# A layout of modes with batches innermost, and mixing matmuls of 64 columns

## The chip, the core and the metric

The kernel runs on one core of one Trainium2 chip. The metric is device time in microseconds for one call: the median of 3 runs is 380.75 us (380.23, 380.75 and 383.44).

## The reference

x is (8, 5696, 128), h (5696, 128), w_r and w_i (64, 128, 128), w_ch (128, 128). First a long convolution of x with h along the sequence, then a spectral mix of the lowest 64 frequencies, then a channel layer with a residual:

```python
# _attn_ref: L = 2 * S
y = irfft(rfft(x, n=L, axis=1) * rfft(h, n=L, axis=0)[None], n=L, axis=1)[:, :S]
# _moe_ref, with x = y of above
X = rfft(x, axis=1);  Xr, Xi = real(X[:, :64]), imag(X[:, :64])
Yr = einsum('bmd,mde->bme', Xr, w_r) - einsum('bmd,mde->bme', Xi, w_i)
Yi = einsum('bmd,mde->bme', Xr, w_i) + einsum('bmd,mde->bme', Xi, w_r)
u = x + irfft(Yr + 1j * Yi on the lowest 64 modes, n=S, axis=1)
return u + maximum(u @ w_ch, 0)
```

## The kernel before, in words

The program is written as one list of operations by a recorder (`R.add`), which keeps for every engine the order in which the operations are recorded and works out the semaphore waits from the buffers and PSUM banks that each one reads and writes. Reads of one PSUM bank by two engines are put in sequence too. So nothing is reordered on an engine: what the code writes first on ScalarE or VectorE runs first there. Matmuls go through `mm` (line 320), evictions of PSUM through `evac` (lines 308 to 314), DMAs through `dma` (line 317).

The sequence is cut into 89 blocks of 64 positions, and the batch into four pairs (`g_`, 0 to 3). The stages in order:

1. 57 warm-up matmuls; then the transform of h along the blocks (`Hp`, `Ah`), and its filter values (`Hs`).
2. For each pair: the transform of x (`a_tile`, written to `As`), and a loop of ticks (`tick`): `second` makes the spectrum from `As` and the table `M`, `products` multiplies it with `Hs`, `third` transforms back in part, evicts to `Zs` or `Zt` and writes that to DRAM (`zscr`), and `modes_of` sums the 64 modes of the mix in PSUM bank 7 (`MB`).
3. At the end of each pair, lines 702 to 705 evict the modes from bank 7 to the tile `XT`. For every batch it has three pieces of 64 columns: minus the imaginary part, the real part, the imaginary part (`XTW` = 192 columns a batch). The first eviction writes the last two pieces for both batches (256 elements a partition), the second the negated one (128). Both are on ScalarE for the first three pairs; in the last, the second is on VectorE.
4. After the last pair, the mix (`mix`, line 773): for each mode m two matmuls with weights of w_r and w_i from the tile `W`, accumulated in PSUM. The moving operand of 16 columns takes, for one mode, two pieces of XT times eight batches, 64 and 192 elements apart. Modes 0 to 31 go to bank 6 and 32 to 63 to bank 7.
5. Between the parts of the mix stand transform matmuls of the output stage that do not need its result (`u_z(..., True)`, 89 columns each, reading `ZT0` and `S4`). They take banks 0 to 5 by the list `LSLOT`. Two reflections (lines 771 and 772), one on VectorE (S4a) and one on ScalarE (S4b), are recorded ahead of the mix.
6. Y is evicted in two halves (line 786): bank 6 on ScalarE, bank 7 on VectorE, 512 elements each. Eight transposes (line 791) turn it, into banks 6 and 7; two evictions write `C`.
7. The output stage: `u_tile` adds C times the table `IBs` (356 columns a matmul) and the transform of `ZT` chunks (five buffers, 1,440 KB a chunk, loaded from `zscr`) to a tile `UT`; `o_tile` makes u @ w_ch next to u, ScalarE the relu, VectorE the sum, SyncE's queue stores it. Chunks are loaded again into a ZT buffer when its matmuls are done.

Of the kernel before, what the change touches and what calls it, by code (L numbers as in the profile page):

```python
# [4 lines left out]
P = 128  # L5
# [8 lines left out]
RELU = mybir.ActivationFunctionType.Relu  # L14
# [109 lines left out]
def bass_long_conv_fft__then__afno_spectral_mix_kernel(nc, x, h, moe_w_r, moe_w_i, moe_w_ch, out):  # L124
    B, S, D = x.shape
    M = moe_w_r.shape[0]
# [122 lines left out]
    XTW = 3 * M  # L249
    xt = at("XT", B * XTW, F16, a_g + GW * 2 + 2048 * (NZX - NZ))  # L250
# [24 lines left out]
    NR = len(r_off)  # L275
    r_sb = [at(f"R{i}", 512, F32, r_off[i]) for i in range(NR)]
    w_sb = at("W", 2 * M * D, F16, a_x)
    y_sb = at("Y", 2 * B * M, F16, r_off[0])
# [10 lines left out]
    def pv(bank, off, dims, p0=0, n=P):  # L289
        return bass.AP(ps, p0 * 4096 + bank * 512 + off, [[4096, n]] + [list(d) for d in dims])  # L290

    R = Recorder(nc)
# [3 lines left out]
    def bank(i):  # L296
        return ("bank", i)
# [3 lines left out]
    def evac(dst, src, reads, writes, scale=None, eng=None, after=()):  # L301
        e = eng
        if e is None:
            turn[0] ^= 1
            e = "scalar" if turn[0] else "vector"
        if e == "scalar":
            if scale is None:
                R.add(e, lambda h_: h_.copy(dst, src), reads, writes, after=after)  # L308
            else:
                R.add(e, lambda h_: h_.activation(dst, src, COPY, scale=scale), reads, writes, after=after)  # L310
        elif scale is None:
            R.add(e, lambda h_: h_.tensor_copy(dst, src), reads, writes, after=after)  # L312
        else:
            R.add(e, lambda h_: h_.tensor_scalar_mul(dst, src, scale), reads, writes, after=after)  # L314
# [4 lines left out]
    def mm(o, l, r, st, sp, reads, writes):  # L319
        R.add("tensor", lambda h_: h_.matmul(o, l, r, start=st, stop=sp), reads, writes)  # L320
# [3 lines left out]
    def once(key, toks):  # L324
        if key in first:
            return []
        first[key] = 1
        return list(toks)
# [72 lines left out]
    MB = 7  # L401
# [14 lines left out]
    for j in range(16):  # L416
        t = turns("h", [0, 2, 4])
        for i in range(8):
            d = 8 * j + i
            for r in range(2):  # L420
# [6 lines left out]
             eng="vector" if j % 4 == 1 else "scalar")  # L427
# [90 lines left out]
    def reflect(eng, t, n, col, key, after):  # L518
        MN = S - SH
        dst, src = bass.AP(t, SH, [[S, n], [1, MN]]), bass.AP(t, SH - NQ - 1, [[S, n], [-1, MN]])  # L520
        sc = sg_sb[0:n, col:col + 1]
        if eng == "scalar":
            R.add(eng, lambda e: e.activation(dst, src, COPY, scale=sc), [key + (0,), ("sg",)], [key + (1,)], after=after)
        else:
            R.add(eng, lambda e: e.tensor_scalar_mul(dst, src, sc), [key + (0,), ("sg",)], [key + (1,)], after=after)
# [153 lines left out]
    for g_ in range(NP):  # L679
        for t in range(NT + LM if g_ + 1 == NP else NT):  # L680
            if g_ == 0 and t % 2 == 0 and t // 2 < NG:
                load_g(t // 2)
            tick(g_, t)
            assert g_ + 1 < NP or not wp
            if g_ == NP - 1 and t in early:
                pace[:] = [("u", min(t, NT - 1) % NU)] if t else []
                early[t]()
        if g_ + 1 < NP:
            load.update(scalar=600.0, vector=0.0)
            third(g_, NT - 2)  # L690
            a_tile(0, [0], share(720))
            a_tile(1, [2], share(720))
            third(g_, NT - 1)
            load["scalar"] += 560.0
            a_tile(2, [0], share(720))
            modes_of(g_, NT - 3)
            a_tile(3, [4], share(720))
            modes_of(g_, NT - 2)
            a_tile(4, [2], share(720))
            modes_of(g_, NT - 1)  # L700
            load["scalar"] += 700.0
        evac(bass.AP(xt, 2 * g_ * XTW + M, [[B * XTW, P], [XTW, 2], [1, P]]), pv(MB, 0, [[P, 2], [1, P]]),
             [bank(MB)], [("xt", g_)], 1.0 / 64, eng="scalar", after=[("ag", k) for k in range(NS + 2 * XN, NK)])
        evac(bass.AP(xt, 2 * g_ * XTW, [[B * XTW, P], [XTW, 2], [1, M]]), pv(MB, M, [[P, 2], [1, M]]),
             [bank(MB)], [("xtn", g_)], -1.0 / 64, eng="vector" if g_ + 1 == NP else "scalar", after=[("ag", k) for k in range(NS + 2 * XN, NK)])
        if g_ + 1 < NP:
            for j in range(5, 32):
                a_tile(j, [(0, 4, 6, 2)[(j - 5) % 4]], "both" if j == 31 else share(720))
                if j == 31:
                    idle(4, 2)  # L710
                if wp and j % 2 == 1:
                    dst, src_, ring, tok = wp.pop(0)
                    dma("gpsimd", dst, src_, ring, (), [tok], after=[("as", j)])
# [56 lines left out]
    XTT = [(n, g_) for g_ in range(NP) for n in ("xt", "xtn")]  # L770
    reflect("vector", s4_sb[0], P, 0, ("s4", 0), M_ALL[1:4])
    reflect("scalar", s4_sb[1], PB + RB, 1, ("s4", 1), AST)
    def mix(m0, m1):
        for m in range(m0, m1):
            for ri, first_col in ((0, M + m), (1, m)):
                mm(pv(6 + m // 32, m % 32 * 2 * B, [[1, 2 * B]]), w_sb[:, (ri * M + m) * D:(ri * M + m + 1) * D],
                   bass.AP(xt, first_col, [[B * XTW, P], [M, 2], [XTW, B]]), ri == 0, ri == 1, WT + XTT, [bank(6 + m // 32)])

    u_z(0, 0, 0, True)
    for n in range(2):  # L780
        mix(16 * n, 16 * n + 16)
        u_z(0, 0, 1, True, (n,))
    mix(32, M)
    u_z(0, 1, 0, True, (0,))
    for hb in range(2):
        evac(bass.AP(y_sb, hb * 32 * B, [[2 * M * B, P], [B, 32], [M * B, 2], [1, B]]),
             pv(6 + hb, 0, [[2 * B, 32], [B, 2], [1, B]]), [bank(6 + hb)], [("y", hb)], eng="vector" if hb else "scalar",
             after=ZY)
    for b in range(B):
        bk = 6 + b // 4  # L790
        R.add("tensor", lambda e, b=b, bk=bk: e.transpose(  # L791
            ps16[:, bk * 1024 + (b % 4) * P:bk * 1024 + (b % 4) * P + P], bass.AP(y_sb, b, [[2 * M * B, P], [B, P]]), id_sb[:, :]),
              [("y", 0), ("y", 1), ("id",)], [bank(bk)])
    u_z(0, 1, 0, True, (1,))
    for hb in range(2):
        evac(c_sb[:, hb * 512:hb * 512 + 512], ps16[:, (6 + hb) * 1024:(6 + hb) * 1024 + 512], [bank(6 + hb)],
# [11 lines left out]
    def o_tile(g_, b, r4):  # L808
        ub = (g_ % 2) * 2 + b
        bb = 2 * g_ + b  # L810
        t = turns("l", LSLOT)
        i = n_o[0]
        n_o[0] += 1
        full = r4 < NW // 4
        last_ = (g_, b) == (NP - 1, 1)
        wide = r4 < (8 if last_ else NW // 4 // 2 * 2)
        big = wide or (last_ and full)
        h_ = r4 % 2 if wide else 0
        if big:
            if not h_:  # L820
                o_cur[0] = turns("o8", list(range(NO8)))
            ob, key, old = o8_sb[o_cur[0]], ("o8", o_cur[0]), o8_old[o_cur[0]]
        else:
            k_ = turns("os", list(range(NO)))
            ob, key, old = o_sb[k_], ("os", k_), o_old[k_]
        OW = 1024 if big else 512
        n, rows = (4, P) if full else (1, TAIL)
        rd = [("u_", ub, c_) for c_ in range(2 * NCH)] + [("wch",), ("i16",)]
        for j in range(n):
            lh = bass.AP(u_sb[ub], 4 * r4 + j, [[S, P], [NW, P]]) if full else u_sb[ub][:, NW * P:S]  # L830
            mm(pv(t + j // 2, (j % 2) * 256, [[1, 256]], 0, rows), lh, WI, True, True, rd, [bank(t + j // 2)])
        bk = [bank(t), bank(t + 1)] if full else [bank(t)]
        rs = r_sb[i % NR]
        rv = bass.AP(rs, 0, [[512, rows], [P, n], [1, P]])
        ov = bass.AP(ob, h_ * 512, [[OW, rows], [P, n], [1, P]])
        src_r, src_u = pv(t, 0, [[256, n], [1, P]], 0, rows), pv(t, P, [[256, n], [1, P]], 0, rows)
        R.add("scalar", lambda e: e.activation(rv, src_r, RELU), bk, [("r", i % NR)], after=once(("r", i % NR), G_ALL + XTT + [("y", 0), ("y", 1), ("id",)]))  # L837
        R.add("vector", lambda e: e.tensor_tensor(ov, src_u, rv, ADD), bk + [("r", i % NR)],  # L838
              [key + (h_,)], after=once(key, old))
        if wide and not h_:  # L840
            return
        w_ = (2 if wide else 1) * 4 * D
        if full:
            dst = bass.AP(out.tensor, out.offset + bb * S * D + (4 * r4 - 4 * h_) * D, [[NW * D, P], [1, w_]])
            src = ob[:, 0:w_]
        else:
            dst = bass.AP(out.tensor, out.offset + bb * S * D + NW * P * D, [[D, TAIL], [1, D]])
            src = ob[0:TAIL, 0:P]
        dma("sync", dst, src, "o", [key + (v_,) for v_ in range(h_ + 1)])
# [53 lines left out]
```

## Time and profile before

| what | before |
|---|---|
| median of 3 runs | 380.75 us (380.23 to 383.44) |
| the profiled execution's own time | 383.51 us |
| its span, first to last instruction | 381.7 us |
| its mean granted TensorE clock | 0.933 |
| busy PE / PEld / DVE / ACT / POOL | 363.6 / 280.4 / 303.7 / 311.9 / 83.9 us |
| the mix: first and last of 128 matmuls start | 257.7 and 262.1 us |
| eviction of Y: ScalarE, VectorE | 585 and 693 ns |
| evictions of XT: 256 elements, 128 elements on ScalarE | 379 and 285 ns (mean) |
| the eight transposes | 263.16 to 264.21 us |
| first and last matmul that reads C (IBs) start | 264.6 and 366.0 us |

The page gives busy time by engine, the span in 40 slices, the chain of work that ended last and the costliest groups. PE is the matmul row, PEld the loading of weights (it overlaps PE), DVE is VectorE, ACT ScalarE, POOL GpSimd, SP SyncE. PEclk is the granted clock of TensorE as a share of full speed. In a line such as `257.70 5.23 PE ps L320 x152` of the chain, the numbers are the start and the length in us, then engine, tile and line, and how many instructions were merged. The times inside the trace are of the profiled execution, which is 2.8 us above the median of the runs.

### The profile page before, as it was taken

To read this page: it belongs to the slowest core of one execution; us is meant where nothing else is said; L and a number is where in the kernel's file an instruction comes from. 1 tells how busy PE (TensorE), PEld (TensorE's weight loads), DVE (VectorE), ACT (ScalarE), POOL (GpSimd) and SP (SyncE) were. 2 spreads that over 40 slices of the span, in tenths; PEclk is the share of its full clock that TensorE was granted. 3 is DMA by queue.
4 is the path that set the end of the run, shared out by engine and by line. 5 is a ranking of instruction groups with operands and counts; after the bars stand their busy time and mean duration, and the time that the engine had idled before them with its cause. 6 is when DMAs were issued, how large, how long until landed. Compare 5 with 4: busy or idle time off the path is not lost.

```text
span 381.7 us, 11950 instructions
## 1 busy us (share of the span) xinstructions
PE 363.6 (95%) x5107; PEld 280.4 (73%) x5107; DVE 303.7 (80%) x331; ACT 311.9 (82%) x492; POOL 83.9 (22%) x137
## 2 busy tenths in 40 slices
PE   7998989999989999999999899999999999999992
PEld 4898856667856667766668666668898988888871
DVE  7566998998988998889998888766347766777784
ACT  8357989998989998999998899994466777777783
POOL 8400012320823311822203211339000000000000
PEclk9997999999999999999999999996899999999997
DMA  7998589998999996999996599999999999999867
GB/s 137 201 280 349 140 228 227 276 269 238 107 134 228 234 269 167 143 129 250 235 283 119 137 298 251 300 328 406 407 388 402 402 415 414 404 408 378 342 256 313
DMA packets 84560, 103.92 MB, mean 272 GB/s; under 512 B 22126, under 2 KB 68974, under 8 KB 81538
## 3 DMA queue, kind: packets, MB, share of 16 engines
q1 hardware_dynamic: 59643, 67.73, 51.3%
q0 software_dynamic: 24864, 35.43, 44.3%
q8 instruction: 40, 0.66, 0.7%
q14 instruction: 13, 0.11, 0.1%
HBM read 70.61 MB, written 51.12 MB: 319 GB/s over the span
## 4 chain that ended last, share of the span: by engine, by line
PE 82%; ACT 9%; DVE 6%; issue 1%; DMA 0%; DVEq 0%
PE ps L320 82%; ACT As L310 7%; DVE As L314 2%; DVE U L597 1%; DVE Hs L312 1%; ACT R L837 0%; DMA F<-cF 0%; DVE UT L312 0%; ACT UT L308 0%; ACT XT L310 0%; DVE O L838 0%; PE ps L791 0%; ACT Hs L308 0%; DVE Os L838 0%; ACT Ah L310 0%
## 5 line engine op out<-in xcount | busy, mean ns | idle before, releaser
L320 PE MATMUL ps<-U,Wc 128*128 128x512 f16 (+1 forms) x368 | 95.8, 384 | 0.0
L605 DVE TENSOR_TENSOR U<-Xs,Hs 128x2048 f16<-128x2048 f16 (+1 forms) x68 | 80.7, 1189 | 11.5 <-ACT Xs L308 10.0
L308 ACT CAST Xs<-ps 128x1024 f16<-128x1024 f32 (+1 forms) x72 | 69.5, 971 | 7.8 <-PE ps L320 4.8
L838 DVE TENSOR_TENSOR O<-ps,R 128x512 f32<-128x512 f32 x81 | 52.5, 686 | 19.8 <-ACT R L837 12.5
L308 ACT CAST Zs<-ps 128x512 f16<-128x512 f32 (+1 forms) x126 | 66.0, 604 | 0.0
L837 ACT ACTIVATE R<-ps 128x512 f32<-128x512 f32 x96 | 50.9, 573 | 14.6 <-PE ps L320 14.1
L314 DVE TENSOR_SCALAR As<-ps 128x720 f16<-128x720 f32 (+1 forms) x60 | 50.1, 879 | 9.1 <-PE ps L320 8.0
L310 ACT ACTIVATE As<-ps 128x720 f16<-128x720 f32 (+1 forms) x72 | 51.6, 772 | 6.6 <-PE ps L320 5.7
L320 PE MATMUL ps<-F,Xin 128*128 128x180 f16 x512 | 54.5, 255 | 2.6 <-ACT Ah L310 1.0
L320 PEld LDWEIGHTS ps<-F,Xin 128*128 128x128 f16 x512 | 46.8, 156 | 9.3 <-DVE As L314 2.6
L320 PE MATMUL ps<-WI,UT 128*128 128x256 f16 x360 | 52.5, 281 | 0.5 <-DVE O L838 0.4
L320 PE MATMUL ps<-As,M 64*128 64x128 f16 x1440 | 48.9, 217 | 4.3 <-DVE U L597 3.5
L320 PEld LDWEIGHTS ps<-U,Wc 128*128 128x128 f16 x368 | 28.5, 98 | 28.5 <-ACT Zs L308 6.1
L320 PEld LDWEIGHTS ps<-As,M 64*128 64x128 f16 x1440 | 40.5, 94 | 10.9 <-DVE U L597 4.2
L317 POOL DMA_DIRECT2D Xt<-in_x_dram x48 | 24.8, 520 | 102.9 <-PE ps L320 102.2
L605 DVE TENSOR_TENSOR U<-ps,Hs 128x2048 f16<-128x2048 f32 x20 | 45.7, 2283 | 0.0
L308 ACT CAST UT<-ps 128x712 f16<-128x712 f32 x40 | 30.0, 752 | 18.7 <-PE ps L320 18.7
L320 PEld LDWEIGHTS ps<-WI,UT 128*128 128x128 f16 x360 | 39.5, 152 | 4.4 <-issue 2.2
L320 PE MATMUL ps<-IBs,C 128*128 128x356 f16 x128 | 40.8, 328 | 0.4
L320 PEld LDWEIGHTS ps<-G,Zs 128*128 128x128 f16 x492 | 27.3, 97 | 13.3
L308 ACT CAST Zt<-ps 128x512 f16<-128x512 f32 (+1 forms) x58 | 31.0, 606 | 0.1
L320 PE MATMUL ps<-G,Zs 128*128 128x2 f16 (+2 forms) x492 | 30.5, 192 | 0.0
(88 smaller groups left out, 500.3 us busy)
## 6 DMA issues: line engine op xcount, KB each, us to landing
out_dram<-O SPq DMA_DIRECT2D x39, 512.0 KB, 10.4
zscr<-Zs SPq DMA_DIRECT2D x60, 256.0 KB, 6.3
Xt<-in_x_dram POOLq DMA_DIRECT2D x24, 320.0 KB, 6.9
zscr<-Zt SPq DMA_DIRECT2D x28, 256.0 KB, 6.6
W<-wscr POOLq DMA_DIRECT2D x8, 512.0 KB, 5.3
M<-cM POOLq DMA_DIRECT2D x5, 720.0 KB, 20.3
ZT0a<-zscr SPq DMA_DIRECT2D x3, 1024.0 KB, 13.4
Xr<-in_x_dram POOLq DMA_DIRECT2D x8, 320.0 KB, 13.8
```

What stands on the lines that cost most here:

```text
L308: R.add(e, lambda h_: h_.copy(dst, src), reads, writes, after=after)
L310: R.add(e, lambda h_: h_.activation(dst, src, COPY, scale=scale), reads, writes, after=after)
L312: R.add(e, lambda h_: h_.tensor_copy(dst, src), reads, writes, after=after)
L314: R.add(e, lambda h_: h_.tensor_scalar_mul(dst, src, scale), reads, writes, after=after)
L317: R.add(eng, lambda h_: h_.dma_start(dst, src), reads, writes, ring=ring, after=after)
L320: R.add("tensor", lambda h_: h_.matmul(o, l, r, start=st, stop=sp), reads, writes)
L597: R.add("vector", lambda e, b=b, s_=s_: e.tensor_tensor(bass.AP(u_s[i], b * 512, [[2048, P], [1024, 2], [1, n * D]]), s_, hv, MULT), [tok, ...
L605: R.add("vector", lambda e: e.tensor_tensor(uv, src, hv, MULT), bk + [("h", t, 0), ("h", t, 1, 0), ("h", t, 1, J)], [("u", i)])
L837: R.add("scalar", lambda e: e.activation(rv, src_r, RELU), bk, [("r", i % NR)], after=once(("r", i % NR), G_ALL + XTT + [("y", 0), ("y", 1 ...
L838: R.add("vector", lambda e: e.tensor_tensor(ov, src_u, rv, ADD), bk + [("r", i % NR)], [key + (h_,)], after=once(key, old))
```

## The change

The tile XT is laid out with batches innermost: each mode has 24 columns, eight for minus the imaginary part, eight for the real part, eight for the imaginary part. The evictions at the end of each pair write the same elements to the new places, so each element lands 48 bytes from the next mode's. A mixing matmul now reads its 16 columns side by side. It reads them four times over (a step of 0) and writes 64 columns, the four copies 64 columns apart in its bank. Only the first copy of a mode is used. Later modes of the same bank write over the copies that lie in their place. The modes are spread over four banks, 4 to 7, 16 modes a bank, instead of two. Y is evicted in quarters, ScalarE and VectorE in turn, each as soon as its 16 modes are recorded, and the transposes wait for all four.

```diff
-        evac(bass.AP(xt, 2 * g_ * XTW + M, [[B * XTW, P], [XTW, 2], [1, P]]), pv(MB, 0, [[P, 2], [1, P]]),
+        evac(bass.AP(xt, 2 * g_ + B, [[B * XTW, P], [1, 2], [B, 2], [3 * B, M]]), pv(MB, 0, [[P, 2], [M, 2], [1, M]]),
...
-        evac(bass.AP(xt, 2 * g_ * XTW, [[B * XTW, P], [XTW, 2], [1, M]]), pv(MB, M, [[P, 2], [1, M]]),
+        evac(bass.AP(xt, 2 * g_, [[B * XTW, P], [1, 2], [3 * B, M]]), pv(MB, M, [[P, 2], [1, M]]),
...
+    MQ = M // 4
+
     def mix(m0, m1):
         for m in range(m0, m1):
-            for ri, first_col in ((0, M + m), (1, m)):
-                mm(pv(6 + m // 32, m % 32 * 2 * B, [[1, 2 * B]]), w_sb[:, (ri * M + m) * D:(ri * M + m + 1) * D],
-                   bass.AP(xt, first_col, [[B * XTW, P], [M, 2], [XTW, B]]), ri == 0, ri == 1, WT + XTT, [bank(6 + m // 32)])
+            for ri, first_col in ((0, B), (1, 0)):
+                mm(pv(4 + m // MQ, m % MQ * 2 * B, [[8 * B, 4], [1, 2 * B]]), w_sb[:, (ri * M + m) * D:(ri * M + m + 1) * D],
+                   bass.AP(xt, m * 3 * B + first_col, [[B * XTW, P], [0, 4], [1, 2 * B]]), ri == 0, ri == 1, WT + XTT, [bank(4 + m // MQ)])
+
+    def y_out(q):
+        evac(bass.AP(y_sb, q * MQ * B, [[2 * M * B, P], [B, MQ], [M * B, 2], [1, B]]),
+             pv(4 + q, 0, [[2 * B, MQ], [B, 2], [1, B]]), [bank(4 + q)], [("y", q)], eng="vector" if q % 2 else "scalar",
+             after=ZY)
 
     u_z(0, 0, 0, True)
     for n in range(2):
-        mix(16 * n, 16 * n + 16)
+        mix(MQ * n, MQ * n + MQ)
+        y_out(n)
         u_z(0, 0, 1, True, (n,))
-    mix(32, M)
+    for n in range(2, 4):
+        mix(MQ * n, MQ * n + MQ)
+        y_out(n)
     u_z(0, 1, 0, True, (0,))
-    for hb in range(2):
-        evac(bass.AP(y_sb, hb * 32 * B, [[2 * M * B, P], [B, 32], [M * B, 2], [1, B]]),
-             pv(6 + hb, 0, [[2 * B, 32], [B, 2], [1, B]]), [bank(6 + hb)], [("y", hb)], eng="vector" if hb else "scalar",
-             after=ZY)
     for b in range(B):
...
-              [("y", 0), ("y", 1), ("id",)], [bank(bk)])
+              [("y", q) for q in range(4)] + [("id",)], [bank(bk)])
```

More of the change, by code (lines that the diff above doesn't have):

```diff
@@ L836, in o_tile @@
         src_r, src_u = pv(t, 0, [[256, n], [1, P]], 0, rows), pv(t, P, [[256, n], [1, P]], 0, rows)
-        R.add("scalar", lambda e: e.activation(rv, src_r, RELU), bk, [("r", i % NR)], after=once(("r", i % NR), G_ALL + XTT + [("y", 0), ("y", 1), ("id",)]))
+        R.add("scalar", lambda e: e.activation(rv, src_r, RELU), bk, [("r", i % NR)], after=once(("r", i % NR), G_ALL + XTT + [("y", q) for q in range(4)] + [("id",)]))
         R.add("vector", lambda e: e.tensor_tensor(ov, src_u, rv, ADD), bk + [("r", i % NR)],
```

## The prediction

> **What bounds the kernel now.** I read the page first. TensorE is busy for 95% of the span and carries 82% of the chain that ended last.
>
> ```profile
> span 381.7 us, 11950 instructions
> PE 363.6 (95%) x5107; PEld 280.4 (73%) x5107; DVE 303.7 (80%) x331; ACT 311.9 (82%) x492; POOL 83.9 (22%) x137
> PEclk9997999999999999999999999996899999999997
> PE 82%; ACT 9%; DVE 6%; issue 1%; DMA 0%; DVEq 0%
> ```
>
> The clock row says more than the busy row: the granted clock dips in slice 4 (about 29 us), in slices 28 and 29 (about 262 us), and at the end, when PE is done. The second dip lies at the mixing stage, which is what the change edits. So next I read the chain of waits from 254 us on, in order of time.
>
> ```profile
> 256.53 1.03 PE ps L320 x18
> 257.56 0.15 issue
> 257.70 5.23 PE ps L320 x152
> 262.93 0.23 issue
> 263.16 1.05 PE ps L791 x8
> 264.21 29.32 PE ps L320 x437
> ```
>
> TensorE is the path without a break: what it loses here, the end loses. The 152 are the 128 mixing matmuls and 24 of the transform; L791 are the eight transposes. Then the view by windows, once per clock window.
>
> ```profile
> 254.80:258.20 3.40, 3.23 (x59) 2.55 (x58) 0.89 (x2) 3.03 (x7) 3.40 (x5) 0.95 1.13 362
> 258.20:261.60 3.40, 3.40 (x113) 3.40 (x110) 2.92 (x1) 2.21 (x2) 3.40 (x4) 0.95 1.05 427
> 261.60:265.00 3.40, 3.17 (x52) 2.85 (x49) 1.45 (x3) 0.60 (x1) 3.40 (x5) 0.50 1.01 398
> 265.00:268.40 3.40, 3.40 (x25) 2.30 (x24) 1.34 (x2) 1.41 (x2) 2.97 (x3) 0.50 1.07 388
> 268.40:271.80 3.40, 3.40 (x64) 3.00 (x63) 1.80 (x2) 1.09 (x2) 0.00 (x0) 0.94 1.05 418
> ```
>
> Columns: stretch, length, busy PE, PEld, DVE, ACT, POOL, granted clock, DMA share, GB/s. From 261.6 to 268.4 us the clock is 0.50 instead of 0.95, though PE was busy for all of the window ahead of it. In the trace's clock records the first dip runs from 29.51 to 32.92 us (3.413 us) and the second from 261.62 to 268.44 (6.827, twice that); they start 232.107 us apart, 68.0 times 3.413. So the clock is decided in steps of 3.413 us.
>
> What decides it? I counted, in each step, the columns that the started matmuls read (their number times their width). 258.2 to 261.6 has 92 of 16 and 16 of 89, that is 2,896, and the clock falls after it. 26.1 to 29.5 has 3,420, and it falls. 254.8 to 258.2 has 4,040, and it stays; every other step between 29.5 and 370 us has more. At half clock, 261.6 to 265.0 has 3,464 and the clock stays low; 265.0 to 268.4 has 3,916 and it rises. So one limit between 3,464 and 3,916 columns per step fits every step of this trace. The mixing matmuls are many but narrow, and fall under it. The view of the tile XT has them:
>
> ```profile
> L320 PE MATMUL ps<-XT,W x128: 187/192/194, 257.7 to 262.1; 128*128 128x16 f16 x128
> L310 ACT ACTIVATE XT<-ps x7: 285/374/383, 94.5 to 256.8; 128x256 f16<-128x256 f32 x4, 128x128 f16<-128x128 f32 x3
> L314 DVE TENSOR_SCALAR XT<-ps x1: 292/292/292, 257.3 to 257.3; 128x128 f16<-128x128 f32 x1
> ```
>
> **Part by part, against the profiled execution's 383.51 us** (span 381.7 and 1.8 around it).
>
> *The mixing matmuls.* Same 128, same weights; 64 columns instead of 16. Start to start they take 29.8 ns now, at either clock, so width does not set it. Rows around it at 0.95: 2 or 4 columns 27 ns, 89 columns 43, 128 columns 55. 64 columns at that clock stream in 28 ns; with the 3 that the 89-wide ones show on top, 31. Cost 128 x 1.2 = +0.15 us; bounds 27 (-0.36) and 43 (+1.7), and I take 31 because the 128-wide row shows no overhead at all.
>
> *The clock.* In the profile's step 258.2 to 261.6 there would be 92 x 64 + 1,424 = 7,312 columns. Ahead of it 4,040 + 18 x 48 = 4,904. Behind it some 18 x 64 + 16 x 89 + 8 x 128 and six of 356, about 5,700. All clear 3,916, so the dip at 261.6 should not come, at whatever phase the steps lie.
>
> *From the last mixing matmul (262.14) to the first that reads C (264.61), 2.47 us now.* The last Y eviction halves: 693 ns for 512 elements on VectorE, 414 for 256 (the Hs eviction's row). Then 0.23 to its start, 0.41, 0.10 to the first transpose, three transposes at 55 instead of 107 ns (0.17), 0.25 until their result is there, 0.60 for C on ScalarE, 0.05: 1.81 us. -0.66. PE's own work in it (8 transposes, 16 of 89 columns) takes about 1.1 and hides.
>
> *From 264.61 to 268.44, at half clock:* 9 matmuls of 356 columns and 16 of 89. Behind the dip they take 154 and 43 ns: 2.07 instead of 3.84 us, -1.77. VectorE's C, IBs reflection and first UT eviction (0.42, 0.93, 0.90 in a row) free banks 0 and 1 about 2.85 us after the first transpose, and PE wants them after 3.0: covered, narrowly.
>
> *Y in four pieces.* All four are waited for by the transposes, and behind these stand all later matmuls. The first lies on ScalarE behind the S4b reflection (ends 259.83), the second on VectorE behind S4a's (ends 261.12); at 0.41 each they are done by 261.6, before the last mixing matmul, and so are banks 4 and 5 for the transform matmuls that now reuse them. Nothing.
>
> *The XT evictions* keep their number and size but write single 2-byte elements 48 bytes apart. Two at each of three boundaries and two at 256.8 are on the chain. Nearest row: As evictions with 4-byte pieces, 512 ns (ACT) and 533 (DVE) for 360 elements, where a line through contiguous rows (Zs 614 for 512, Xs 1017 for 1024) gives 494: 4% more. At 4%, +0.06 us in all. Upper bound: the element part doubles, 0.3 per boundary, +1.2. Nothing suggests a gain.
> [...]
>
> *What is late next.* DMA share is 1.0 from 255 to 345 us, so transfers do not come earlier with PE. ZT3b lands at 273.64 and is first read at 276.37; ZT4b 277.63 and 280.31: 2.7 us to spare. PE about 2 us earlier uses that up, and the reload of ZT0 (issued 268.34 when PE has freed it) starts 2 us sooner and shares the engines with them. 0 to +1.0; I take +0.3.
>
> Sum: 0.15 - 0.66 - 1.77 + 0.06 + 0.3 = -1.92: the profiled execution would take 381.6.
>
> **From there to the median.** The profiled execution is 2.8 us above the median of 380.75, beside the highest run (383.44). Two things depend on where the steps fall: whether the gap near 28.5 to 29.5 brings the early dip (the change leaves it alone), and how long the later dip lasts. The narrow stretch (about 255.4 to 262.3) is longer than a step, so each phase has at least one low step; the dip's end then falls between 265.7 and 269.1. Each us behind 264.61 costs 1.77/3.84 = 0.46, so the clock term lies between 0.5 and 2.1. The lower runs are likelier short dips: end at 266.5, 0.87, with 0.1 for DMA. 0.15 - 0.66 - 0.87 + 0.06 + 0.1 = -1.2. Forecast 379.5 us.
>
> **Rivals.**
> *The clock falls all the same (slower).* The trace shows columns with a clock, not that a column read four times counts four times. If only new data or results count, the mixing step still has 2,896 and the dip stays; but now 64 columns at half clock take 53 ns (half of the transposes' 107), 23.5 more than now. The dip starts between 258.9 and 262.3 by phase, so 10 to 100 of the 128 pay: +0.2 to +2.3, less 0.28 for Y. It decides as soon as the counted columns stay below 3,464. Middle: 381.8. Against it, from the trace: the 57 warm-up matmuls read 180 columns twice each; the step up to 5.62 us has 11 of them, 3,960 columns in full and 1,980 if a repeat counts nothing, and the clock rose. For it: those were twice, these are four times 16, and a count of another kind that fits all steps is not excluded.
> [...]
>
> *The dip goes, but transfers hide the gain.* ZT3b and ZT4b come late by a us: 379.5 + 0.9 = 380.4. For it: the DMA share of 1.0. Against: 2.7 us to spare.
>
> *XT's writes cost their double.* 379.5 + 1.1 = 380.6. For it: no row has pieces of 2 bytes. Against: pieces of 4 bytes cost 4%. [...]
>
> *More than forecast.* If the timed runs carry the long dip and the steps after it never dip again, the gain is 2.5 to 3, and with luck in the early dip 376.5.
>
> **How the numbers follow.** Forecast 0.62 (378.2 to 380.0), clock falls 0.10, transfers 0.08, XT 0.08, more 0.12. The range from 377.4 to 382.0 leaves out the best of the last and the worst of the first rival. About 1% (3.8 us) is what a measurement of this kernel can tell from no change. Faster by more needs 376.9 or less: most of "more" and a little of the forecast, 0.15. Slower by more needs 384.6: the first rival's end with dear XT writes, 0.05. Within: 0.80.
>
> **What would show it.** Clock 0.95 throughout 258 to 272 us, mixing at about 31 ns start to start, the first IBs matmul some 0.5 us sooner after the mix, XT evictions near 390 ns, no wait of PE for ZT. Wrong if the clock row still dips there, or if XT evictions near 600 ns stand in the chain.

## The result and the profile after

The changed kernel takes 383.88 us (median of 10 runs, 382.67 to 385.03); the kernel before, in the runs beside it, 380.33 (10 runs, 379.15 to 383.44). The ratio is 1.0085, 95% interval 1.006 to 1.011: slower by 0.6 to 1.1%, where 0.3% faster was forecast. The time lies outside the forecast range.

The page of the changed kernel, the lines that answer to those of before:

```profile
span 380.9 us, 11952 instructions
PE 358.1 (94%) x5107; PEld 275.4 (72%) x5107; DVE 302.1 (79%) x332; ACT 316.0 (83%) x493; POOL 84.1 (22%) x137
PEclk9999999999999999999999999999999999999998
PE 75%; ACT 12%; DVE 6%; DMA 5%; issue 1%; SPq 0%; DVEq 0%
```

The clock's dip at the mix is gone, as forecast. PE's share of the chain fell from 82 to 75%, and ScalarE's rose from 9 to 12. The second of these belongs to the change, the first does not: the second profile of the kernel before, below, has 73 and 10%, as its chain too passes through a late load at the end. The chain in order of time says what ScalarE added (start, length, what):

```profile
92.69 0.78 ACT As L310
93.47 1.82 ACT XT L310 x2
95.30 0.05 issue
...
149.28 1.83 ACT XT L310 x2
...
205.08 1.83 ACT XT L310 x2
...
258.59 1.35 ACT XT L310
259.95 0.94 issue
260.89 4.91 PE ps L320 x152
265.80 0.23 issue
266.03 0.45 PE ps L797 x4
266.48 0.02 issue
266.50 0.61 ACT C L310
267.11 0.05 issue
267.15 26.36 PE ps L320 x424
```

The two XT evictions at the end of a pair are 1.82 us of the chain, three times. Before they were 0.44:

```profile
94.64 0.44 ACT XT L310 x2
149.47 0.44 ACT XT L310 x2
204.30 0.44 ACT XT L310 x2
```

At the end of the last pair 2.3 us lie between the first XT eviction and the first mixing matmul (258.59 to 260.89), before 0.88. The "issue" (time in which the profile shows no wait) at 259.95 covers the VectorE eviction of XT, which the chain does not tell. The view of the tile XT (min, median and max in ns, over both sizes) has the same by instruction:

```profile
L320 PE MATMUL ps<-XT,W x128: 190/193/194, 260.9 to 265.3; 128*128 128x64 f16 x128
L310 ACT ACTIVATE XT<-ps x7: 1117/1340/1347, 93.4 to 258.6; 128x256 f16<-128x256 f32 x4, 128x128 f16<-128x128 f32 x3
L314 DVE TENSOR_SCALAR XT<-ps x1: 746/746/746, 260.0 to 260.0; 128x128 f16<-128x128 f32 x1
```

Same number and size of instructions, but 1340 ns instead of 376 for 256 elements on ScalarE, and 746 instead of 292 for 128 on VectorE. The windows around the mix:

```profile
258.20:261.60 3.40, 1.82 (x45) 1.59 (x44) 1.56 (x2) 3.03 (x3) 3.40 (x3) 1.00 1.06 406
261.60:265.00 3.40, 3.40 (x116) 3.40 (x112) 1.71 (x2) 1.58 (x3) 3.40 (x6) 1.00 1.03 418
265.00:268.40 3.40, 3.07 (x52) 2.43 (x49) 2.08 (x4) 1.03 (x2) 3.40 (x4) 1.00 1.04 392
```

The granted clock is 1.00 through the mix and behind it; PE is idle ahead of it (busy for 1.82 of 3.40 us), for XT. It is 1.00 here where the first profile of the kernel before had 0.95. The second profile of that kernel, below, has 1.00 too, so this is no part of the change, and what follows compares with the second one.

### The profile page after: what moved, and what is told of

Same layout as the page of the kernel before. It is cut to its first block, busy times and chain, and to the rows that moved or that the text cites. A ratio compares the mean times of both kernels' runs of the same rounds, so it can differ in the third digit from the quotient of the medians.

```text
span 380.9 us, 11952 instructions
## 1 busy us (share of the span) xinstructions
PE 358.1 (94%) x5107; PEld 275.4 (72%) x5107; DVE 302.1 (79%) x332; ACT 316.0 (83%) x493; POOL 84.1 (22%) x137
## 4 chain that ended last, share of the span: by engine, by line
PE 75%; ACT 12%; DVE 6%; DMA 5%; issue 1%; SPq 0%; DVEq 0%
PE ps L320 75%; ACT As L310 7%; DMA ZT0b<-zscr 4%; DVE As L314 3%; ACT XT L310 2%; DVE U L597 1%; ACT R L843 1%; ACT UT L308 1%; DVE Hs L312 1%; DMA F<-cF 0%; DVE UT L312 0%; DVE O L844 0%; SPq L317 0%; ACT Hs L308 0%; DVE Os L844 0%
## 5 line engine op out<-in xcount | busy, mean ns | idle before, releaser
L320 PE MATMUL ps<-U,Wc 128*128 128x512 f16 (+1 forms) x368 | 94.4, 376 | 0.0
L320 PE MATMUL ps<-F,Xin 128*128 128x180 f16 x512 | 52.8, 249 | 6.9 <-ACT XT L310 4.6
L310 ACT ACTIVATE As<-ps 128x720 f16<-128x720 f32 (+1 forms) x72 | 52.5, 787 | 5.7 <-PE ps L320 5.0
L320 PEld LDWEIGHTS ps<-F,Xin 128*128 128x128 f16 x512 | 45.0, 155 | 13.8 <-ACT XT L310 5.1
L320 PE MATMUL ps<-IBs,C 128*128 128x356 f16 x128 | 39.3, 314 | 0.7
```

## The experiments

**The kernel before, again.**

> The kernel before, unchanged, for a second look at its clock. If the clock is decided by columns per step of 3.41 us, the granted clock falls to 0.5 in or behind the mixing stage again, for two or three steps, and XT evictions take 376 and 285 ns. If the dip of the first profile was chance, the clock stays up through the mix.

379.41 us, a single run. The clock fell at the end of the mix for one step (259.5 to 262.9 us; two or three were expected), XT's evictions took 376 and 285 ns.

```profile
PEclk9999999999999999999999999998999999999998
PE 73%; ACT 10%; DMA 7%; DVE 6%; issue 1%; SPq 0%; DVEq 0%; POOL 0%
L310 ACT ACTIVATE XT<-ps x7: 284/376/383, 93.3 to 254.4; 128x256 f16<-128x256 f32 x4, 128x128 f16<-128x128 f32 x3
```

With it the account of the two traces closes. The changed kernel loses 4.15 us up to the first matmul on ZT0 (three pairs' ends) and 1.41 from there to the first mixing matmul. It gains 0.07 in the mix, 0.57 from its last matmul to the first with IBs, 0.33 over the next 24 of these, and 1.18 from there to the last of them. That is +3.41; the end behind it is 0.15 shorter, and the spans differ by 3.3.

**The new matmuls on the old layout.** XT as before, the 16 scattered columns read four times:

```diff
-        evac(bass.AP(xt, 2 * g_ + B, [[B * XTW, P], [1, 2], [B, 2], [3 * B, M]]), pv(MB, 0, [[P, 2], [M, 2], [1, M]]),
+        evac(bass.AP(xt, 2 * g_ * XTW + M, [[B * XTW, P], [XTW, 2], [1, P]]), pv(MB, 0, [[P, 2], [1, P]]),
...
-                   bass.AP(xt, m * 3 * B + first_col, [[B * XTW, P], [0, 4], [1, 2 * B]]), ri == 0, ri == 1, WT + XTT, [bank(4 + m // MQ)])
+                   bass.AP(xt, first_col, [[B * XTW, P], [0, 4], [M, 2], [XTW, B]]), ri == 0, ri == 1, WT + XTT, [bank(4 + m // MQ)])
```

> The changed kernel with XT in the layout of before: the evictions write contiguous pieces again, and the mixing matmul reads 16 scattered columns four times over. Theory (the scattered 2-byte writes of XT are the whole loss, 1.4 us at each of four places): evictions 376 and 285 ns, clock high through the mix, 383.9 - 5.6 = 378.3 us, faster than before by some 2 us. Rival (the 64-column mix, its four banks or Y in quarters cost the time): about 383 to 384. Second rival (scattered reads of 64 columns slow the mix): mixing matmuls well over 31 ns start to start.

389.58 us; the ratio to the kernel before, run beside it, is 1.0262 (1.0235 to 1.0289). My first theory got the evictions right and the time wrong; the second rival was true. In the view of the tile XT of this run:

```profile
L320 PE MATMUL ps<-XT,W x128: 268/288/293, 255.3 to 270.2; 128*128 128x64 f16 x128
L310 ACT ACTIVATE XT<-ps x7: 285/374/383, 93.4 to 254.4; 128x256 f16<-128x256 f32 x4, 128x128 f16<-128x128 f32 x3
```

The mix lasts 14.9 us instead of 4.4: 110 ns a matmul, start to start, for 64 scattered columns, at full and at half clock, against 29 for 64 of which 16 lie side by side. So the scattered read costs 1.7 ns a column. The clock fell as well (1.00 from 256.2 to 259.6 us, 0.50 from 259.6 to 266.4), for four steps of some 1,900 to 2,500 columns each: the matmuls were wide, but slow. On the old layout the copies cost time.

**The new layout on the old matmuls.** The two evictions as in the changed kernel, 16 columns read once, two banks, Y in halves.

> The kernel before with only the new layout of XT: scattered writes, 16 contiguous columns read once, two banks, Y in halves. Theory (the writes are the loss): 380.3 + 5.6 = 385.9 us, evictions 1340 and 1120 ns, clock falls to 0.5 behind the mix as in the kernel before. Rival (the layout is not what costs): 380 to 381.

385.76 us, ratio 1.0159 (1.0117 to 1.0202), forecast 385.9: 6.0 us above the kernel before beside it, where 5.6 were expected. The layout alone, without its copies:

```profile
L320 PE MATMUL ps<-XT,W x128: 169/174/221, 260.8 to 265.0; 128*128 128x16 f16 x128
L310 ACT ACTIVATE XT<-ps x7: 1112/1337/1347, 93.3 to 258.5; 128x256 f16<-128x256 f32 x4, 128x128 f16<-128x128 f32 x3
L314 DVE TENSOR_SCALAR XT<-ps x1: 744/744/744, 259.9 to 259.9; 128x128 f16<-128x128 f32 x1
```

The evictions cost what they cost in the changed kernel, and the clock fell in the mix (1.00 up to 262.7 us, 0.50 from there to 266.1), for two steps. The matmul of 16 columns side by side takes 25 ns at full clock instead of 30.

**The same layout, written in pairs.** Only the order changes in which each eviction goes through its elements: the two batches of a pair, side by side in XT, come one right after the other.

```diff
-        evac(bass.AP(xt, 2 * g_ + B, [[B * XTW, P], [1, 2], [B, 2], [3 * B, M]]), pv(MB, 0, [[P, 2], [M, 2], [1, M]]),
+        evac(bass.AP(xt, 2 * g_ + B, [[B * XTW, P], [3 * B, M], [B, 2], [1, 2]]), pv(MB, 0, [[1, M], [M, 2], [P, 2]]),
...
-        evac(bass.AP(xt, 2 * g_, [[B * XTW, P], [1, 2], [3 * B, M]]), pv(MB, M, [[P, 2], [1, M]]),
+        evac(bass.AP(xt, 2 * g_, [[B * XTW, P], [3 * B, M], [1, 2]]), pv(MB, M, [[1, M], [P, 2]]),
```

> The changed kernel with the same layout of XT, but the evictions go through the elements in another order: the two batches that lie side by side are written one right after the other, so that 4 bytes go to one place, and PSUM is read with a step. Theory A (a lone 2-byte write is what costs): evictions 380 to 450 ns, about 378.5 us. [...] Theory C (the bytes' distance does not matter, a pattern of this many steps does): 1100 ns or more, about 384 us.

379.65 us (12 runs), ratio to the kernel before 0.999 (0.9971 to 1.0009). That is 4.2 us under the 383.88 of the changed kernel, or 3.6 by the ratios of the two to the kernel before, as they were measured at different times.

```profile
L320 PE MATMUL ps<-XT,W x128: 189/193/193, 255.1 to 259.5; 128*128 128x64 f16 x128
L310 ACT ACTIVATE XT<-ps x7: 285/401/417, 93.1 to 254.2; 128x256 f16<-128x256 f32 x4, 128x128 f16<-128x128 f32 x3
L314 DVE TENSOR_SCALAR XT<-ps x1: 291/291/291, 254.7 to 254.7; 128x128 f16<-128x128 f32 x1
```

The same bytes in the same places for 401 to 417 ns (256 elements) instead of 1340. Theory A's number, and the PSUM read with a step of 512 bytes is in it: both together cost 25 to 41 ns. So the order of its writes was the whole loss of the change. But 378.5 was expected, and the kernel is level with the one before, although the clock stays high in its trace (a mean of 0.999). That is the second question.

**Other distances of a lone write.** The kernel before with XT in two more layouts, in which single elements land 4 and then 8 bytes apart (the longer of the two evictions is shown; the matmuls read what it writes):

```diff
-        evac(bass.AP(xt, 2 * g_ * XTW + M, [[B * XTW, P], [XTW, 2], [1, P]]), pv(MB, 0, [[P, 2], [1, P]]),
+        evac(bass.AP(xt, 2 * g_ * XTW + 2 * M, [[B * XTW, P], [1, 2], [2 * M, 2], [2, M]]), pv(MB, 0, [[P, 2], [M, 2], [1, M]]),
```

```diff
-        evac(bass.AP(xt, 2 * g_ * XTW + M, [[B * XTW, P], [XTW, 2], [1, P]]), pv(MB, 0, [[P, 2], [1, P]]),
+        evac(bass.AP(xt, (g_ // 2) * 4 * XTW + (g_ % 2) * 2 + 4 * M, [[B * XTW, P], [1, 2], [4 * M, 2], [4, M]]), pv(MB, 0, [[P, 2], [M, 2], [1, M]]),
```

> The kernel before (16 columns, read once) with a third layout of XT: modes side by side with the two batches of a pair interleaved, so that the evictions write single 2-byte elements 4 bytes apart instead of 48. [...] The mixing matmul reads 8 pieces of 4 bytes: between 25 ns (one piece) and 30 ns (16 pieces) start to start.

> [...] 48 bytes apart took 1340 ns for 256 elements, 4 bytes apart 457, side by side 376. [...]

The tile XT at 4 bytes:

```profile
L310 ACT ACTIVATE XT<-ps x7: 315/447/479, 93.8 to 255.1; 128x256 f16<-128x256 f32 x4, 128x128 f16<-128x128 f32 x3
L314 DVE TENSOR_SCALAR XT<-ps x1: 304/304/304, 255.7 to 255.7; 128x128 f16<-128x128 f32 x1
```

and at 8 bytes:

```profile
L310 ACT ACTIVATE XT<-ps x7: 555/730/756, 93.6 to 256.1; 128x256 f16<-128x256 f32 x4, 128x128 f16<-128x128 f32 x3
L314 DVE TENSOR_SCALAR XT<-ps x1: 446/446/446, 256.9 to 256.9; 128x128 f16<-128x128 f32 x1
```

For 256 elements: 376 side by side, about 460 at 4 bytes, 745 at 8 (730 to 756), 1340 at 48. At 8 bytes neither of my estimates came (400 to 550, not far above the price side by side, or 860, half of the extra at 48 bytes). So a lone 2-byte write is not dear as such (theory A as I had put it fell: by it 4 bytes would have cost 1340 too), and the price grows with the distance over these three. In the pairs the same 256 elements cost about 410: written right behind its neighbour an element is nearly free, though the next pair lies 48 bytes on. Why that is so is not shown. The times, 380.92 and 382.33 us, are single runs.

**Where the clock's gain goes.** First, with pairs, fewer copies: two as here, and then one, without this dimension.

```diff
-                mm(pv(4 + m // MQ, m % MQ * 2 * B, [[8 * B, 4], [1, 2 * B]]), w_sb[:, (ri * M + m) * D:(ri * M + m + 1) * D],
-                   bass.AP(xt, m * 3 * B + first_col, [[B * XTW, P], [0, 4], [1, 2 * B]]), ri == 0, ri == 1, WT + XTT, [bank(4 + m // MQ)])
+                mm(pv(4 + m // MQ, m % MQ * 2 * B, [[8 * B, 2], [1, 2 * B]]), w_sb[:, (ri * M + m) * D:(ri * M + m + 1) * D],
+                   bass.AP(xt, m * 3 * B + first_col, [[B * XTW, P], [0, 2], [1, 2 * B]]), ri == 0, ri == 1, WT + XTT, [bank(4 + m // MQ)])
```

> The changed kernel with XT written in pairs and the 16 columns read twice instead of four times (32 columns a matmul). The limit of 3,464 to 3,916 columns a step says: 92 x 32 + 16 x 89 = 4,368 in the mixing step, so the clock stays high, as with four copies; if only distinct columns counted, or the limit lay higher, it falls to 0.5 behind the mix. 16 side by side took 25 ns start to start, 64 took 29: 32 should take 25 to 27, 0.3 to 0.5 us less in all than four copies, 379.2 us if transfers let it through, 379.6 if they do not.

> The changed kernel with XT written in pairs, four banks and Y in quarters, but the 16 columns read once. What is left against the run with four copies is the clock alone: it should fall behind the mix for one to three steps. 25 to 27 ns a matmul instead of 29 (-0.4 us), and 0.9 to 1.8 us more up to the first 24 matmuls with IBs. If transfers hide the clock's gain, the time is within 0.4 of the run with four copies, 379.6 to 380; if they do not, 380.5 to 381.

380.61 us, ratio 0.9999 (0.9972 to 1.0027), and 379.95, ratio 0.9989 (0.9967 to 1.001). For two copies 379.2 to 379.6 had been expected. Both matmuls take 25 ns. With two copies the clock held (a mean of 0.997 in the profiled execution). With one it held too in the profiled execution, at 3,469 columns in the step of the mix; the mean clock of its 12 runs is 0.992 at the median, like that of the kernel before beside it (0.990), against 0.996 for two and four copies. So it seems to fall in most of these runs, though no record says where, and it makes no difference that their times can show. What took the gain in the run with two copies, by the view of waits (who waited for whom, us, times, longest), 255 to 345 us:

```profile
PE ps L320 <- DVE O L844: 1.6, 1, 1.6
PE ps L320 <- DVE UT L312: 0.6, 1, 0.6
PE ps L320 <- DMA ZT0b<-zscr: 0.4, 1, 0.4
```

PE waits for a bank that VectorE empties late, because its output buffer is not stored yet (VectorE itself waits 2.6 us for that store), and for ZT0b; both are transfers. The 0.6 us for UT are VectorE's own. With four copies and pairs PE waited for ZT0b (0.6 us). But in the second profile of the kernel before it did too, and longer (1.0), so these waits do not tell by themselves where a gain goes.

Then I moved transfers. On GpSimd's queue, the loads of ZT3 and ZT4 ahead of the memsets:

```diff
-                  NT - 2: lambda: (load_ib(), load_zt(1, "gpsimd", SLACK), load_zt(2, "gpsimd"), clear_zt(1), clear_zt(2))}
+                  NT - 2: lambda: (load_ib(), load_zt(1, "gpsimd", SLACK), load_zt(2, "gpsimd"))}
...
-    load_wi()
     for i in range(3, NC):
         load_zt(i, "gpsimd")
+    clear_zt(1)
+    clear_zt(2)
+    load_wi()
+    for i in range(3, NC):
         clear_zt(i)
```

> The changed kernel with XT written in pairs, and on GpSimd's queue the loads of ZT3 and ZT4 moved ahead of the memsets of ZT1b and ZT2b and the load of WI (they are issued some 3 and 4 us sooner). Theory (the clock's gain of 1.8 us is given back where ZT3b, ZT4b and at last ZT0b land just in time): the slack of ZT3b and ZT4b, 0.8 and 0.5 us, grows to 2 or more, and the wait for ZT0b near 342 us stays, so about 379.2. Rival (the engines are full, so that an earlier issue lands no earlier): slack as it was, 379.6.

379.85 us, ratio 0.9989 (0.9964 to 1.0015). The rival was true: ZT3b was issued 5.2 us sooner (254.43 instead of 259.65) and landed 0.6 sooner (270.25 instead of 270.87). Its slack, from landing to first use, stayed at 0.8. And, on top of that, the last reload on GpSimd's queue:

```diff
-                load_zt(i + NC)
+                load_zt(i + NC, "gpsimd" if i + NC == NB - 1 else "sync")
```

> The run with loads first, and besides the last reload (chunk 15, ZT0a and ZT0b) issued from GpSimd's queue instead of SyncE's, where it lands behind the output stores. Theory (the last wait is that transfer, 16 to 17 us from issue to landing): it lands 3 us or more sooner, PE does not wait for ZT0b, 378.3 to 378.8, faster than both kernels. Rival (all 16 engines are full, or the stores come late instead): 379.2 to 380.

384.24 us, ratio 1.0085 (1.0055 to 1.0115): slower, which neither theory had. ZT0b landed at 333.0, 14 us ahead of its use. But the waits between 325 and 345 us were:

```profile
DVE O L847 <- DMA out_dram<-O: 4.5, 1, 4.5
PE ps L320 <- DVE O L847: 4.5, 2, 3.4
```

The stores came late instead: VectorE waited 4.5 us for an output buffer, and PE 4.5 in two waits for VectorE. The place in the queues chose who waited, and here the new wait was the longer one (4.5 us, where PE had waited 1.0 for ZT0b).

Last, I took transfers away, in pairs of kernels. Halved stores leave half of the output unwritten, in the kernel before and with pairs:

```diff
-        w_ = (2 if wide else 1) * 4 * D
+        w_ = (2 if wide else 1) * 2 * D
```

> The kernel before, but each store of 128 rows to the output takes only the first half of its columns (half of the output is not written). It is the base for the next run: with some 11 MB less to move, transfers are no limit in the output stage. PE then waits for no ZT; the time falls by the wait for ZT0b and the last store, 1 to 3 us, to 377 to 379.

> The changed kernel with XT written in pairs, with the same halved stores. Theory (the clock's gain is there, but transfers hide it at ZT0b near 342 us): against the run before it, 1.2 to 2.2 us less, where with full stores the two differ by 0.15. Rival (the clock in these runs costs little, since the dip of before is short): still only 0 to 0.5 us less.

377.81 and 377.58 us; the ratios to the kernel before, 0.9933 (0.9908 to 0.9957) and 0.9923 (0.99 to 0.9946), overlap. The rival's 0 to 0.5 us came. It does not settle the question: PE of the second still waited 0.6 us for ZT3b, which PE of the first did not. Without the reloads, so that later work reads the first ZT tiles again, only stores are left behind the first loads:

```diff
-            if b == 1 and i + NC < NB:
-                load_zt(i + NC)
```

> The kernel before without the reloads of ZT: chunks 5 to 15 are computed from what the first five loads left, so most of the output is not the reference's. Some 15 MB less is moved in the output stage, stores are the only stream there. It is the base of the next run. 1 to 3 us under the kernel before: 377 to 379.

> The run with XT in pairs and loads first, without the reloads of ZT in the same way. Theory (full transfer engines take back what the clock and the shorter Y path gain): without them the gain of 0.6 (Y path) and 0.9 to 1.8 (clock) reaches the end, so 1.3 to 2.2 us less than the run before it, outside both intervals. Rival (something else in the output stage sets its pace, VectorE or ScalarE): still within 0.5 us of it.

378.73 and 376.72 us, ratios 0.9955 (0.9929 to 0.9981) and 0.991 (0.9876 to 0.9945). The means are 378.84 (12 runs) and 376.92 (6): 1.9 us apart, with a standard error of 0.4. So most of the gain appears once these transfers are gone. (The ratios' intervals still overlap at their ends, and the second kernel also has the loads first, which changed nothing with the reloads in place; without them that was not tried by itself.) The windows view of this last kernel,

```profile
284.00:300.00 16.00, 15.91 (x232) 14.21 (x230) 11.65 (x19) 11.47 (x21) 0.00 (x0) 1.00 0.55 222
320.00:341.00 21.00, 20.79 (x285) 18.26 (x283) 16.20 (x26) 15.27 (x28) 0.00 (x0) 1.00 0.60 241
```

and of the same with full reloads (the run with pairs),

```profile
284.00:300.00 16.00, 15.91 (x231) 14.21 (x228) 11.70 (x18) 11.29 (x21) 0.00 (x0) 1.00 1.00 396
320.00:341.00 21.00, 20.91 (x288) 18.43 (x284) 16.07 (x25) 15.24 (x28) 0.00 (x0) 1.00 1.00 406
```

show the DMA share at 0.55 to 0.60 in one and at 1.00 in the other, with PE just as busy in both.

The traces bear this out only in part. From the first matmul on ZT0 to the last eviction of output, the second profile of the kernel before takes 119.72 us and the run with pairs 118.60, so in this execution, the fastest of its 12 (378.01 us), 1.1 us of the gain did arrive with all transfers in place. Without the reloads it is 118.45 and 117.25, 1.2 us. Behind that eviction the end follows after 3.4 to 3.6 us in some executions with full stores and after 4.9 to 5.3 in others, the kernel before among both (5.23 and 3.61), so single spans differ by some 1.7 us for a reason other than the change. That the transfers take the gain therefore rests on the median times, and how they do it is not shown.

## Why the prediction was wrong, point by point

**XT's evictions: the step that failed.** "At 4%, +0.06 us in all. Upper bound: the element part doubles [...] +1.2." They cost 1.39 us at each of three boundaries and 1.41 at the last: 5.6 us, and the element part did not double but took six times as long (1340 and 376 ns, less about 190 that do not depend on the size, by the 376 ns for 256 elements and 285 for 128). The sum had a term of 0.06 where 5.6 belonged, and its upper bound was 1.2. The row I leaned on was the wrong neighbour. As evictions write 4 bytes to a place, that is, a pair; the pairs run shows that this is just the case that is nearly free (about 410 ns for 256 elements, 376 side by side). No row of the trace had a lone 2-byte write far from the next, so the upper bound should not have been a doubling; the widest price that the trace shows for a scattered access was in the mixing matmul itself, 30 ns for 16 columns where 27 were shown for 2 or 4, and I did not ask why.
The rival "XT's writes cost their double" had the right place and a fifth of the size (1.1 us of the 5.6). The doubling was my estimate; no run shows one.

**The clock.** Right in its direction. It stays high through the mix in all six traces with four copies on the new layout (1.00 in the changed kernel from 258.2 to 268.4 us): the rival "the clock falls all the same" fell. (In the run with pairs the step at 255.8 us has 7,376 columns, 2,912 without the repeats.) From the first matmul with IBs to the 24th after it, the first profile of before took 11.58 us, at half clock for 3.8 of it, and the changed kernel 9.77: 1.81 less, where 1.77 was worked out. That the two agree so well is the luck of this execution: in the seven traces with the narrow matmuls whose clock fell at the mix, this stretch was 0.33 to 1.81 us longer than 9.77. That "one limit between 3,464 and 3,916 columns" fits was too neat: counted over all traces of this case, steps of 2,896 and fewer among matmuls lost the clock each time. Between 3,144 and 3,600 both happened: in the first profile of before it fell to 0.50 behind a step of 3,420, at 29.5 us, and in the changed kernel it stayed at 1.00 behind steps of 3,144 and 3,420, at 95.6 and 208.2 us. With 3,676 and more it stayed or came back, with one exception: in the run with the last reload on GpSimd's queue it fell from 16.6 to 23.5 us, behind a step of 5,220 columns and with 5,130 in each step of the dip.

```profile
PEclk9879999999999999999999999999999999999998
```

So the columns of a step went with the clock here but do not settle it, and what decides it, and what brought that dip, is not shown.

**Mix and Y.** The mix cost 0.07 less instead of 0.15 more (29.1 ns a matmul against 29.8): the scattered read of before had made 16 columns as slow as 64. From the last mixing matmul to the first with IBs: -0.57 against the second profile of before, -0.58 against the first, forecast -0.66.

**"Covered, narrowly"** (VectorE's C, IBs reflection and UT) held in the changed kernel, but not in four others: with pairs, with pairs and half stores, with two copies and with one, PE waited 0.2 to 0.7 us for that bank.

**Transfers.** The rival "transfers hide the gain" was priced at 0.9 us. For the versions without XT's cost the medians speak for it: 0.15 us is left of the 1.9 that clock and shorter Y path together gave without the reloads. In the changed kernel itself the wait for ZT0b is 0.3 us; with 1.4 us more ahead of the mix, the loads are that much further.

## What to carry to other kernels

When a layout makes one side's access contiguous, look at what the other side then does element by element, and choose the order of its access pattern so that neighbours in memory are written one after the other: here that was worth about 4 us for the same bytes in the same places. Narrow matmuls went with a clock of 0.50 here (behind a step of 2,896 columns), and with their columns read four times (7,376) it stayed at 1.00; but before that is worked for, ask whether the stage behind has room: here 1.9 us of gain showed without the reloads and 0.15 with them. A price "between" two rows of a trace is only safe if the new operation has the property that made those rows cheap.

## What the hardware showed that I had not expected

- An eviction of 256 f16 elements on ScalarE takes 376 ns side by side, about 410 in pairs 48 bytes apart, about 460 singly 4 bytes apart, 745 at 8 and 1340 at 48; on VectorE, 128 elements take 291, 291, 304, 446 and 745.
- TensorE pays for scattered columns too: 16 moving columns take 25 ns side by side, 25 in eight pairs (the run with 4 bytes) and 30 scattered, 64 take 29 (16 of them side by side, read four times) and 110 (scattered).
- The granted clock outside the dips was 0.95 in the first profile of the kernel before and 1.00 in every later one, yet matmuls of 356 columns started 153 ns apart in that profile and in the changed kernel's, and those of 89 columns 43 and 42 to 43. Matmuls of 512 columns did show it, 224 ns apart at 0.95 and 216 at 1.00, and 0.50 cost far more (296 ns for 356 columns).
